# A two-matmul SiLU block on one core: first rows of x and first columns of w1 in smaller, interleaved pieces

## The chip, the core and the metric

The kernel runs on one core of one Trainium2 chip. The core has five engines with a program of their own each: TensorE (PE in the profile, its weight loads PEld), VectorE (DVE), ScalarE (ACT), GpSimd (POOL) and SyncE (SP). They meet only at semaphores. DMAs are issued from SP's and ACT's programs into one queue each (q1 and q10 in the profile). The metric is the device time of one execution in microseconds; lower is better.

## The reference

`x` is 1 x 2048 x 640, `w1` is 640 x 1728, `w2` is 1728 x 640, all bfloat16:

```python
def reference(x, w1, w2):
    h = jnp.einsum("bsd,df->bsf", x, w1)
    h = _silu(h)                      # h * sigmoid(h)
    out = jnp.einsum("bsf,fd->bsd", h, w2)
    return out
```

## The kernel before

TensorE contracts over the partitions, so the first product needs x transposed: 640 = 5 slices (DT) of 128 contraction rows. The 1728 columns of w1 are 13 full column blocks of 128 (ft 0 to 12) and a tail of 64. The 2048 rows of x are four chunks (sc) of 512.

**Getting x transposed.** Chunks 1 to 3 are transposed by the DMA itself (line 224, five per chunk, on SP's queue). Chunk 0 would come too late that way: its 512 rows are loaded as they are into x0_sb (line 206 on SP: rows 0 to 255; line 401 on ACT: rows 256 to 511), and TensorE transposes them by a matmul with the identity, in row blocks j of 128, five matmuls each (line 295). DVE copies three of a block's five results to xT_sb (line 468), ACT the other two (line 416).

**Loading w1.** In four groups of column blocks, 0-1, 2-3, 4-7 and 8-13. Group 0 is issued by ACT behind x's second half (line 406), groups 1 to 3 by SP (line 213), after SP has waited until x's first half has landed. SP then waits for group 2 before it issues the transposes, with the loads of w2 behind those of chunk 2.

**Warm-up.** TensorE first runs nine 512-column matmuls on z_sb, a tile of zeros (line 277), whose halves POOL (line 184) and DVE (line 463) write; it waits for both. Then it waits for POOL's identity.

**First product.** A unit is one column block times 512 rows: five accumulating matmuls (line 350) into one of four PSUM banks; ACT takes the sigmoid (line 426), DVE multiplies it with the sum and writes hT_sb, h transposed (line 490). In chunk 0, column blocks 0 and 1 are taken in two halves of 256 rows, first both blocks for rows 0 to 255, then both for the rest; the others take 512 rows. The 64-column tails of two chunks share one unit (line 339, lines 426 and 481), after chunks 1 and 3. On each engine the units are in one order.

**Second product.** For each of 16 row tiles of 128, 14 pairs of matmuls (line 388), 512 and 128 output columns wide; DVE copies the 512 (line 503), ACT the 128 (line 438) to one of four output buffers, SP stores (line 259). The last two tiles are taken together: first both of their 512-column parts, copied by DVE (line 515) and stored by SP (line 265), then both of their 128-column parts, copied by ACT (line 450) and stored by ACT (line 455).

The order of the work is written out by hand per engine, with a semaphore count at each wait. SP's head:

```python
            sp.wait_ge(sem_x0[0], 16)
            for gi in range(N_W1_ACT, len(w1_groups)):
                load_w1_group(gi)
```

Of the kernel before, what the change touches and what calls it, by code (L numbers as in the profile page):

```python
# [6 lines left out]
ALU = mybir.AluOpType  # L7


def bass_standalone__dense_activation_silu__prompt_kernel(  # L10
# [13 lines left out]
    P = 128  # L24
    assert D % P == 0 and S % 512 == 0 and 512 < D <= 1024
    DT = D // P
    FT = (F + P - 1) // P
    FP = FT * P
    F_LAST = F - (FT - 1) * P
    ST = S // P  # L30
    SCH = 512
    NSC = S // SCH
    JB = SCH // P
    NB1 = 4
    NOB = 4
    DA = 512
    DB = D - DA
    assert ST >= 4 and ST % 2 == 0 and (ST - 2) % NOB + 1 == (ST - 1) % NOB
    assert JB % 2 == 0

    w1_groups = [(0, 2), (2, 4), (4, 8), (8, FT)]
    N_W1_ACT = 1
    W1_BIG = 2

    def w1_group_of(ft):
        for gi, (a, b) in enumerate(w1_groups):
            if a <= ft < b:
                return gi
        raise AssertionError

    HN = SCH // 2
    N_SPLIT_FT = 2
    units = []
    for ft in range(N_SPLIT_FT):
        units.append((0, ft, 0, HN))
    for ft in range(N_SPLIT_FT):
        units.append((0, ft, HN, HN))
    PACK_TAIL = (F_LAST <= 64) and (FT >= 2)
    FT_REG = FT - 1 if PACK_TAIL else FT
    for ft in range(N_SPLIT_FT, FT_REG):  # L60
        units.append((0, ft, 0, SCH))
    for sc in range(1, NSC):
        for ft in range(FT_REG):
            units.append((sc, ft, 0, SCH))
        if PACK_TAIL and sc % 2 == 1:
            units.append((-1, sc - 1, sc, 0))
    if PACK_TAIL and NSC % 2 == 1:
        units.append((-1, NSC - 1, None, 0))
    NU = len(units)

    def unit_chunks(u):
        if u[0] == -1:
            return [c for c in (u[1], u[2]) if c is not None]
        return [u[0]]

    dve_incs = [len(unit_chunks(u)) if u[0] == -1 else 1 for u in units]
    dve_val = []
    acc = 0
    for inc in dve_incs:
        acc += inc  # L80
        dve_val.append(acc)
    chunk_done_cnt = {}
    for i, u in enumerate(units):
        for c in unit_chunks(u):
            chunk_done_cnt[c] = dve_val[i]
    def tail_half(sc):
        if not PACK_TAIL:
            return 0
        if NSC % 2 == 1 and sc == NSC - 1:
            return 0  # L90
        return sc % 2

    n_w2_full = FT - 1 if F_LAST != P else FT
    w2_half = n_w2_full // 2
    n_w2_dmas = (4 if (F - (FT - 1) * P) <= 64 else 3) if n_w2_full != FT else 2
    N_INIT = 3 + (1 if (not PACK_TAIL and FP != F) else 0)
    N_PAD = 1 if (PACK_TAIL or FP != F) else 0
    N_WARM_MM = 9
    TPV = 3
    assert TPV <= 4 and DT - TPV <= 4  # L100

    TP_BANKS = {0: (1, 0), 1: (1, 8), 2: (0, 8), 3: (1, 0)}

    def tp_slot(j, dt):
        which, base = TP_BANKS[j % 4]
        slot = base + dt if dt < TPV else base + 4 + (dt - TPV)
        return which, slot

    with ExitStack() as es:
# [3 lines left out]
        def ps(name, shape, dtype):  # L113
            return es.enter_context(nc.psum_tensor(name, shape, dtype))

        def sem(name):
            return es.enter_context(nc.semaphore(name))

        xT_sb = sb("xT_sb", [P, DT, S], bf16)
        w1_sb = sb("w1_sb", [P, DT, FP], bf16)  # L120
        w2_sb = sb("w2_sb", [P, FT, D], bf16)
        hT_sb = sb("hT_sb", [P, FT, S], bf16)
        sig_sb = sb("sig_sb", [P, NB1, SCH], bf16)
        o_sb = sb("o_sb", [P, NOB, D], bf16)
# [3 lines left out]
        z_sb = sb("z_sb", [P, SCH], bf16)  # L128
        ps1 = ps("ps1", [P, NB1, SCH], fp32)
        ps2 = ps("ps2", [P, 2, 1024], fp32)  # L130
        tp_views = [
            ps1[:, :, :].rearrange("p a (k s) -> p (a k) s", s=P),
            ps2[:, :, :].rearrange("p a (k s) -> p (a k) s", s=P),
        ]

        sem_init = sem("sem_init")
        sem_w2pad = sem("sem_w2pad")
        sem_z = sem("sem_z")
        sem_x0 = [sem(f"sem_x0_{i}") for i in range(JB // 2)]
        sem_x = [None] + [sem(f"sem_x{i}") for i in range(1, NSC)]  # L140
        sem_w1 = [sem(f"sem_w1_{i}") for i in range(len(w1_groups))]
        sem_w2 = sem("sem_w2")
        sem_o = [sem(f"sem_o{i}") for i in range(NOB)]
        sem_tp = sem("sem_tp")
        sem_tpc_v = sem("sem_tpc_v")
        sem_tpc_a = sem("sem_tpc_a")
        sem_pe1 = sem("sem_pe1")
        sem_act1 = sem("sem_act1")
        sem_dve1 = sem("sem_dve1")
        sem_pe2 = sem("sem_pe2")  # L150
        sem_ev_v = sem("sem_ev_v")
        sem_ev_a = sem("sem_ev_a")
        sem_ofin = sem("sem_ofin")
        block = es.enter_context(nc.Block())
# [3 lines left out]
        w2_full_v = w2[0:n_w2_full * P, :].rearrange("(ft p) d -> p ft d", p=P)  # L158

        segs = []  # L160
        for st in range(ST - 2):
            b2 = st % 2
            segs.append([(st, 0, b2, 0, DA), (st, 1, b2, DA, DB)])
        sA, sB = ST - 2, ST - 1
        segs.append([(sA, 0, 0, 0, DA), (sB, 0, 0, 512, DA)])
        segs.append([(sA, 1, 1, 0, DB), (sB, 1, 1, 512, DB)])
        grp_order = []
        for seg in segs:
            for g in seg:
                grp_order.append((g[0], g[1]))  # L170
        grp_idx = {g: i + 1 for i, g in enumerate(grp_order)}
        seg_done_idx = {}
        for seg in segs:
            last = max(grp_idx[(g[0], g[1])] for g in seg)
            for g in seg:
                seg_done_idx[(g[0], g[1])] = last
        grp_loc = {}
        for seg in segs:
            for (st, ci, b2, c0, ncol) in seg:
                grp_loc[(st, ci)] = (b2, c0, ncol)  # L180

        @block.gpsimd
        def _(pool):
            pool.memset(z_sb[:, SCH // 2:SCH], 0.0).then_inc(sem_z, 1)  # L184
            pool.memset(ident[:, :], 0.0).then_inc(sem_init, 1)
            pool.wait_ge(sem_init, 1)
            pool.affine_select(
                out=ident[:, :],
                in_=ident[:, :],
                compare_op=ALU.not_equal,  # L190
                fill=1.0,
                base=0,
                pattern=[[-1, P]],
                channel_multiplier=1,
            ).then_inc(sem_init, 1)
            pool.memset(warm_sb[:, :], 0.0).then_inc(sem_init, 1)
            if PACK_TAIL:
                pool.memset(hT_sb[:, FT - 1, :], 0.0).then_inc(sem_w2pad, 1)  # L198
            elif FP != F:
                pool.memset(w1_sb[:, :, F:FP], 0.0).then_inc(sem_init, 1)  # L200
                pool.memset(w2_sb[:, FT - 1, :], 0.0).then_inc(sem_w2pad, 1)

        @block.sync
        def _(sp):
            hj = JB // 2
            sp.dma_start(
                out=x0_sb[:, 0:hj, :], in_=x0_v[:, 0:hj, :]
            ).then_inc(sem_x0[0], 16)

            def load_w1_group(gi):  # L210
                a, b = w1_groups[gi]
                f0, f1 = a * P, min(b * P, F)
                sp.dma_start(
                    out=w1_sb[:, :, f0:f1], in_=w1_v[:, :, f0:f1]
                ).then_inc(sem_w1[gi], 16)

            sp.wait_ge(sem_x0[0], 16)
            for gi in range(N_W1_ACT, len(w1_groups)):
                load_w1_group(gi)

            def x_chunk_transposes(sc):
                s0 = sc * SCH
                for dt in range(DT):
                    sp.dma_start_transpose(
                        out=xT_sb[:, dt, s0:s0 + SCH],
                        in_=xf[s0:s0 + SCH, dt * P:(dt + 1) * P],
                    ).then_inc(sem_x[sc], 16)

            sp.wait_ge(sem_w1[W1_BIG], 16)
            for sc in range(1, NSC):  # L230
                x_chunk_transposes(sc)
                if sc == min(2, NSC - 1):
                    sp.dma_start(
                        out=w2_sb[:, 0:w2_half, :], in_=w2_full_v[:, 0:w2_half, :]
                    ).then_inc(sem_w2, 16)
                    sp.dma_start(
                        out=w2_sb[:, w2_half:n_w2_full, :],
                        in_=w2_full_v[:, w2_half:n_w2_full, :],
                    ).then_inc(sem_w2, 16)
                    if n_w2_full != FT:  # L240
                        if PACK_TAIL:
# [305 lines left out]
```

## Time and profile before

| what | value |
|---|---|
| time, median of 3 runs | 130.99 us (130.43 to 130.99) |
| span of the profiled execution | 128.5 us (the page has no other time of that execution) |
| PE busy | 124.7 us, 97%, 767 matmuls |
| DVE / ACT busy | 52.1 us / 39.5 us |
| first product (lines 350 and 339) | 6.17 to 64.99 us |
| second product (line 388) | 64.99 to 125.97 us |
| DMA | 9.87 MB, 77 GB/s over the span |

The span runs from the first to the last instruction; the times of runs also hold what lies around it. A line of the timeline has the start, the duration, the engine, the line of the kernel, the operation, output <- input, their shapes and, in brackets, the idle time before it with what ended it; merged instructions have a count xN, and their duration goes from the first start to the last end. A line of the chain has start, duration and what ran. Matmuls are pipelined, so the duration of one is its latency; how far apart they start says how fast they go. Times of DMA issues are from the start of the issuing instruction to the moment when the semaphore shows the data landed.

### The profile page before, as it was taken

Reading aid. Unit: us, or ns where it says so; the run is one execution under the profiler, and the core shown is the slowest. Engines: PE = TensorE matmul, PEld = TensorE weight load, DVE = VectorE, ACT = ScalarE, POOL = GpSimd, SP = SyncE. Lnnn points to the kernel's source line nnn. Section 1 sums busy time; section 2 is a strip of 40 time slices with the busy share of each in tenths; the row PEclk is TensorE's granted clock in tenths of the full one; section 3 lists DMA queues with packets and bytes.
Section 4 is the critical chain, followed back from the end, with each engine's and each line's share of the span. In section 5 each row is a group of like instructions: output and inputs, shape, how many; then the busy total and the mean of one; then the engine's idle time right before and its main releaser. Section 6 shows DMA issues by size and latency. Waiting matters only on the chain.

```text
span 128.5 us, 1884 instructions
## 1 busy us (share of the span) xinstructions
PE 124.7 (97%) x767; PEld 63.9 (50%) x767; DVE 52.1 (41%) x78; ACT 39.5 (31%) x77; POOL 2.8 (2%) x9
## 2 busy tenths in 40 slices
PE   6999999999999999999999999999999999999992
PEld 2574444444444444444455555555555555555461
DVE  0475666666676666666662210222220122221021
ACT  4355555555555555555520000000000000000001
POOL 7000000000000000000000000000000000000000
PEclk9999999999999999999999999999999999999999
DMA  3897463599900000000000111111011111011103
GB/s 100 258 367 207 109 96 87 98 355 347 195 8 5 0 3 0 0 0 0 0 5 15 36 51 51 56 51 48 3 51 51 56 51 51 12 39 56 51 0 102
DMA packets 15752, 9.87 MB, mean 77 GB/s; under 512 B 8832, under 2 KB 15744, under 8 KB 15744
## 3 DMA queue, kind: packets, MB, share of 16 engines
q1 hardware_dynamic: 14544, 9.03, 24.8%
q10 hardware_dynamic: 1200, 0.72, 1.8%
q8 instruction: 6, 0.10, 0.3%
q14 instruction: 2, 0.02, 0.0%
HBM read 5.16 MB, written 2.62 MB: 61 GB/s over the span
## 4 chain that ended last, share of the span: by engine, by line
PE 97%; ACT 1%; POOL 0%; issue 0%; POOLq 0%
PE ps L388 47%; PE ps L350 44%; PE ps L277 3%; PE ps L339 2%; PE ps L295 1%; ACT xT_sb L416 1%; ACT o_sb L450 0%; POOL z_sb L184 0%; POOLq L532 0%
## 5 line engine op out<-in xcount | busy, mean ns | idle before, releaser
L388 PE MATMUL ps<-w_sb,hT_sb 128*128 128x512 bf16 (+1 forms) x448 | 61.0, 299 | 0.0
L350 PE MATMUL ps<-xT_sb,w_sb 128*128 128x512 bf16 (+1 forms) x270 | 56.5, 371 | 0.0
L388 PEld LDWEIGHTS ps<-w_sb,hT_sb 128*128 128x128 bf16 x448 | 34.4, 98 | 26.8 <-issue 0.4
L490 DVE TENSOR_TENSOR hT_sb<-ps,sig_sb 128x512 bf16<-128x512 f32 (+1 forms) x54 | 36.3, 672 | 19.9 <-ACT sig_sb L426 19.4
L350 PEld LDWEIGHTS ps<-xT_sb,w_sb 128*128 128x128 bf16 x270 | 26.2, 98 | 29.9 <-issue 0.4
L426 ACT ACTIVATE sig_sb<-ps 128x512 bf16<-128x512 f32 (+1 forms) x56 | 32.6, 582 | 26.5 <-PE ps L350 25.3
L503 DVE CAST o_sb<-ps 128x512 bf16<-128x512 f32 x14 | 9.7, 692 | 42.3 <-PE ps L388 42.3
L438 ACT CAST o_sb<-ps 128x128 bf16<-128x128 f32 x14 | 3.7, 266 | 49.3 <-PE ps L388 49.3
L277 PE MATMUL ps<-z_sb 128*128 128x512 bf16 x9 | 3.4, 557 | 1.1 <-POOL z_sb L184 1.1
L468 DVE CAST xT_sb<-ps 128x384 bf16<-128x384 f32 x4 | 1.9, 549 | 4.1 <-PE ps L295 4.1
L515 DVE CAST o_sb<-ps 128x1024 bf16<-128x1024 f32 x1 | 1.2, 1225 | 5.4 <-PE ps L388 5.4
L481 DVE TENSOR_TENSOR hT_sb<-ps,sig_sb 64x512 bf16<-64x512 f32 x4 | 2.8, 689 | 1.1 <-ACT sig_sb L426 1.0
L450 ACT CAST o_sb<-ps 128x256 bf16<-128x256 f32 x1 | 0.4, 373 | 7.3 <-PE ps L388 7.3
L277 PEld LDWEIGHTS ps<-z_sb 128*128 128x128 bf16 x9 | 1.1, 136 | 2.9 <-issue 1.8
L339 PE MATMUL ps<-xT_sb,w_sb 128*64 128x512 bf16 x20 | 2.5, 384 | 0.0
L416 ACT CAST xT_sb<-ps 128x256 bf16<-128x256 f32 x4 | 1.3, 373 | 1.9 <-PE ps L295 1.9
L410 ACT ACT_TABLE_LOAD x1 | 1.3, 1283 | 1.8 <-issue 1.8
L198 POOL MEMSET hT_sb<- 128x2048 bf16 x1 | 1.8, 1805 | 0.0
L339 PEld LDWEIGHTS ps<-xT_sb,w_sb 128*64 128x64 bf16 x20 | 1.0, 109 | 1.5 <-issue 0.8
L295 PE MATMUL ps<-ident,x_sb 128*128 128x128 bf16 x20 | 1.4, 219 | 0.2 <-ACT xT_sb L416 0.2
L295 PEld LDWEIGHTS ps<-ident,x_sb 128*128 128x128 bf16 x20 | 1.1, 97 | 0.8 <-issue 0.5
L463 DVE MEMSET z_sb<- 128x128 uint32 x1 | 0.2, 165 | 0.8 <-PEq L532 0.8
(9 smaller groups left out, 1.6 us busy)
## 6 DMA issues: line engine op xcount, KB each, us to landing
out_dram<-o_sb SPq DMA_DIRECT2D x14, 160.0 KB, 1.8
w_sb<-in_w_dram SPq DMA_DIRECT2D x1, 1120.0 KB, 8.1
w_sb<-in_w_dram SPq DMA_DIRECT2D x1, 960.0 KB, 5.6
w_sb<-in_w_dram SPq DMA_DIRECT2D x1, 880.0 KB, 7.2
w_sb<-in_w_dram SPq DMA_DIRECT2D x1, 640.0 KB, 5.5
x_sb<-in_x_dram SPq DMA_DIRECT2D x1, 320.0 KB, 3.7
x_sb<-in_x_dram ACTq DMA_DIRECT2D x1, 320.0 KB, 4.0
w_sb<-in_w_dram ACTq DMA_DIRECT2D x1, 320.0 KB, 4.5
```

The source lines that it names most:

```text
L277: pe.matmul(ps1[:, NB1 - 1, :], lhsT=z_sb[:, 0:P], rhs=z_sb[:, :], start=True, stop=True,)
L295: ins = pe.matmul(tp_views[wv][:, sl, :], lhsT=x0_sb[:, j, dt * P:(dt + 1) * P], rhs=ident[:, :], start=True, stop=True,)
L339: ins = pe.matmul(ps1[hh * 64:hh * 64 + F_LAST, buf, :], lhsT=w1_sb[:, dt, f0:f0 + F_LAST], rhs=xT_sb[:, dt, scc * SCH:(scc + 1) * SCH], s ...
L350: ins = pe.matmul(ps1[:, buf, 0:n], lhsT=w1_sb[:, dt, ft * P:(ft + 1) * P], rhs=xT_sb[:, dt, col0:col0 + n], start=(dt == 0), stop=(dt == ...
L388: ins = pe.matmul(ps2[:, b2, c0:c0 + ncol], lhsT=hT_sb[:, ft, st * P:(st + 1) * P], rhs=w2_sb[:, ft, d0:d0 + ncol], start=(ft == 0), stop= ...
L416: act.copy(out=xT_sb[:, TPV:DT, j * P:(j + 1) * P], in_=tp_views[wv][:, s0_:s0_ + (DT - TPV), :],).then_inc(sem_tpc_a, 1)
L426: act.activation(out=sig_sb[:, buf, 0:n], in_=ps1[:, buf, 0:n], func=ACT.Sigmoid,).then_inc(sem_act1, 1)
L438: act.copy(out=o_sb[:, ob, DA:D], in_=ps2[:, b2, c0:c0 + ncol]).then_inc(sem_ev_a, 1)
L468: dve.tensor_copy(out=xT_sb[:, 0:TPV, j * P:(j + 1) * P], in_=tp_views[wv][:, s0_:s0_ + TPV, :],).then_inc(sem_tpc_v, 1)
L481: dve.tensor_tensor(out=hT_sb[hh * 64:hh * 64 + F_LAST, FT - 1, scc * SCH:(scc + 1) * SCH], in0=ps1[hh * 64:hh * 64 + F_LAST, buf, :], in1 ...
L490: dve.tensor_tensor(out=hT_sb[:, ft, col0:col0 + n], in0=ps1[:, buf, 0:n], in1=sig_sb[:, buf, 0:n], op=ALU.mult,).then_inc(sem_dve1, 1)
L503: dve.tensor_copy(out=o_sb[:, ob, 0:DA], in_=ps2[:, b2, c0:c0 + ncol]).then_inc(sem_ev_v, 1)
```

## The change

The whole program is written anew as a list of operations, each with its engine and the operations it depends on; a small planner gives each engine its operations in list order, with a wait for every dependence that an earlier wait has not covered. The computation is the same. What differs:

- Warm-up: six matmuls instead of nine, on a constant of ones that exists before the kernel's own first instruction, without a wait. z_sb is gone.
- Loads: x's rows 0 to 127 on SP, rows 128 to 255 on ACT, then on SP w1 group 0, w1 group 1, x's rows 256 to 511, w1 groups 2 and 3. SP waits for none of them before it issues the next. The DMA transposes wait for w1 group 2, as before.
- Order on TensorE in chunk 0: row blocks 0 and 1 transposed; column blocks 0 and 1 for rows 0 to 127, then for rows 128 to 255 (matmuls of 128 columns); column block 2 for rows 0 to 255; row blocks 2 and 3 transposed; column block 3 for rows 0 to 255; column blocks 0 to 3 for rows 256 to 511; the other blocks with 512 rows. DVE, ACT follow in the same order.
- PSUM is one tile of eight banks, taken in turn by transposes, units and output tiles; the second of the two transposed pieces of a row block has its own bank. There were four banks for units, and two pairs for output tiles.
- o_sb holds all 16 output tiles; nothing waits for a store but the end.
- w1_sb has 1728 columns instead of 1792.

```diff
-        @block.sync
...
-            sp.dma_start(
-                out=x0_sb[:, 0:hj, :], in_=x0_v[:, 0:hj, :]
-            ).then_inc(sem_x0[0], 16)
...
-            sp.wait_ge(sem_x0[0], 16)
-            for gi in range(N_W1_ACT, len(w1_groups)):
-                load_w1_group(gi)
...
-            sp.wait_ge(sem_w1[W1_BIG], 16)
-            for sc in range(1, NSC):
-                x_chunk_transposes(sc)
...
-            pe.wait_ge(sem_z, 2)
-            for i in range(N_WARM_MM):
...
-            for j in range(JB):
-                transpose_block(j)
...
+class Plan:
...
+        def run(name, eng):
+            seen = {}
+            for op in self.ops:
+                if op.eng != name:
+                    continue
+                need = {}
+                for d in op.deps:
+                    need[d.sem] = max(need.get(d.sem, 0), d.value)
+                for s, v in need.items():
+                    if seen.get(s, 0) < v:
+                        eng.wait_ge(sems[s], v)
+                        seen[s] = v
+                ins = op.emit(eng)
+                if op.sem is not None:
+                    ins.then_inc(sems[op.sem], 16 if op.group else 1)
...
+        load_x0("sp", 0, 1)
+        load_x0("act", 1, 2)
+        load_w1("sp", 0)
+        load_w1("sp", 1)
+        load_x0("sp", 2, 4)
+        load_w1("sp", 2)
+        load_w1("sp", 3)
+        add("act", lambda e: e.activation(out=warm_sb[:, :], in_=warm_sb[:, :], func=ACT.Sigmoid), [warm])
+
+        ones = nc.const_aps.tensor(1.0, [P, SCH], bf16)
+        for i in range(N_WARM):
+            add("pe", lambda e: e.matmul(
+                ps[:, NBANK - 1, :], lhsT=ones[:, 0:P], rhs=ones, start=True, stop=True))
...
+        def transpose_x0(j):
+            b0, b1 = take_bank(), take_bank()
+            for dt in range(DT):
+                b, k = (b0, dt) if dt < TPV else (b1, dt - TPV)
+                deps = [x0_of[j], id_b] + bank_free[b]
+                pe = add("pe", lambda e, b=b, k=k, dt=dt: e.matmul(
+                    ps[:, b, k * P:(k + 1) * P], lhsT=x0_sb[:, j, dt * P:(dt + 1) * P],
+                    rhs=ident[:, :], start=True, stop=True), deps)
+            cols = slice(j * P, (j + 1) * P)
+            v = add("dve", lambda e: e.tensor_copy(
+                out=xT_sb[:, 0:TPV, cols],
+                in_=ps[:, b0, 0:TPV * P].rearrange("p (k s) -> p k s", s=P)), [pe])
+            a = add("act", lambda e: e.copy(
+                out=xT_sb[:, TPV:DT, cols],
+                in_=ps[:, b1, 0:(DT - TPV) * P].rearrange("p (k s) -> p k s", s=P)), [pe])
+            bank_free[b0], bank_free[b1] = [v], [a]
+            xT_ready[0, j] = [v, a]
...
+        def unit(sc, ft, c0, n):
+            b = take_bank()
+            cols = slice(sc * SCH + c0, sc * SCH + c0 + n)
+            for dt in range(DT):
+                pe = add("pe", lambda e, dt=dt: e.matmul(
+                    ps[:, b, 0:n], lhsT=w1_sb[:, dt, ft * P:(ft + 1) * P], rhs=xT_sb[:, dt, cols],
+                    start=(dt == 0), stop=(dt == DT - 1)),
+                    x_deps(sc, c0, n) + w1_deps(ft) + bank_free[b] if dt == 0 else ())
+            silu(b, [(slice(0, P), ft, cols)], n, pe)
...
+        transpose_x0(0)
+        transpose_x0(1)
+        for c in range(2):
+            for ft in range(2):
+                unit(0, ft, c * P, P)
+        unit(0, 2, 0, 2 * P)
+        transpose_x0(2)
+        transpose_x0(3)
+        unit(0, 3, 0, 2 * P)
+        for ft in range(4):
+            unit(0, ft, 2 * P, 2 * P)
+
+        for ft in range(4, FR):
+            unit(0, ft, 0, SCH)
```

## The prediction

> **What bounds the kernel now.** I read the chain that ended last first, in order of time. It is TensorE nearly from end to end:
>
> ```profile
> 1.10 3.44 PE ps L277 x9
> 4.54 0.45 PE ps L295 x5
> 5.02 0.66 ACT xT_sb L416 x2
> 5.71 0.45 PE ps L295 x5
> 6.17 28.26 PE ps L350 x140
> 34.43 1.20 PE ps L339 x10
> 35.63 28.16 PE ps L350 x130
> 63.79 1.20 PE ps L339 x10
> 64.99 60.97 PE ps L388 x448
> ```
>
> From 6.17 us to 125.97 us matmuls follow one another without a gap; in the groups by line, L350, L339 and L388 have 0.0 us idle before them. A change can win only in the 6.17 us ahead of the first real matmul, by making the stream shorter, or after its end. The stream keeps the same columns, and the end is unchanged. So I read the head next, by the timeline:
>
> ```profile
> 0.83 0.17 DVE L463 MEMSET z_sb<- 128x128 uint32 x1 [0.83 <-PEq L532]
> 1.93 0.15 PEld L277 LDWEIGHTS ps<-z_sb 128*128 128x128 bf16 x1 [0.28 <-issue]
> 2.36 0.15 PEld L277 LDWEIGHTS ps<-z_sb 128*128 128x128 bf16 x1 [0.28 <-issue]
> 4.54 1.00 PE L295 MATMUL ps<-ident,x_sb 128*128 128x128 bf16 x15
> 5.09 1.95 DVE L468 CAST xT_sb<-ps 128x384 bf16<-128x384 f32 x4 [4.09 <-PE ps L295]
> 7.34 2.06 DVE L490 TENSOR_TENSOR hT_sb<-ps,sig_sb 128x256 bf16<-128x256 f32 x4 [0.30 <-ACT sig_sb L426]
> 10.38 6.83 SPq L224 DMA_TRANSPOSE xT_sb<-in_x_dram  x5
> ```
>
> Warm-up matmuls start 0.43 us apart, half of full speed, until the last two (3.95 against 3.64 for their weight loads): the slow clock ended near 4.0 us, although the granted-clock column reads 1.00 throughout. At full clock a 128-column matmul takes 57 ns (15 in 1.00 us), a 256-column one 110 ns (20 in 2.2 us), a 512-column one 217 ns. Transposes began at 4.54; the copies of two row blocks on DVE, about 0.5 us each, gave the first unit at 6.17, 1.63 us later.
>
> Then the DMA issues, whose last column is the time from issue to landing:
>
> ```profile
> w_sb<-in_w_dram SPq DMA_DIRECT2D x1, 880.0 KB, 7.2
> w_sb<-in_w_dram SPq DMA_DIRECT2D x1, 640.0 KB, 5.5
> x_sb<-in_x_dram SPq DMA_DIRECT2D x1, 320.0 KB, 3.7
> x_sb<-in_x_dram ACTq DMA_DIRECT2D x1, 320.0 KB, 4.0
> w_sb<-in_w_dram ACTq DMA_DIRECT2D x1, 320.0 KB, 4.5
> w_sb<-in_w_dram SPq DMA_DIRECT2D x1, 320.0 KB, 3.2
> ```
>
> With issue times 0.74 (x, both), 1.25, 4.42, 4.9 and 5.4 us, x's halves land at 4.42 and 4.74, w1's groups at 5.75, 7.6, 10.4 and 12.6. The queues' packets in quarter-microsecond windows give when bytes stopped moving: SP's x at 3.95 (landing 0.45 later), ACT's x at 4.0 (0.7), w1 group 0 at 5.2 (0.55), group 1 at 6.85 (0.75), group 2 at 8.75 (1.63). So the lag between bytes and landing grows in a stream that stays full.
>
> **The change part by part.** Let T be when the second half of the first 512 rows (rows 256 to 511) is transposed and copied. Before, the first chunk's units end at 6.17 + 2.20 (four 256-column units) + 11 x 1.086 = 20.32 us. After, T is followed by four 256-column units (2.20) and nine full ones (9.77): the end is T + 11.97. Break-even is T = 8.35 us, and from there on the two kernels do the same.
>
> *Warm-up.* Its operand is a constant written ahead of the starting barrier, so it starts when DVE's first instruction did, 0.83 instead of 1.10. Six at 0.427 end at 3.4. z_sb's two memsets (0.31 and 0.17 us) go; the identity, finished at 1.7 before, comes earlier; all of that lies beside the loads. On ACT the function-table load (1.28 us, at 1.79 before) moves up behind a single DMA issue and is over by about 2.8, ahead of its first copy at 4.15.
>
> *First loads.* The first 128 rows go alone on SP. SP's first 124 packets had moved by 2.75, so 128 by 2.8; with lag 0.45 to 0.7 they land at 3.25 to 3.5, about when the warm-up ends. The second 128 rows, on ACT's queue, land near 3.9 (117 of ACT's packets by 3.5). Five transposes at half clock (107 ns) from 3.4, then the copy: DVE starts 4.15, ends 4.7; the second copy ends about 5.25. Group 0 of w1 now sits on SP behind 160 KB; 640 KB in all had moved by 4.0 before, and 512-byte rows move at 346 GB/s, so 4.2 plus lag 0.55: 4.75. First unit at 4.8, a lead of 1.37 us.
>
> *Narrow pieces.* 20 matmuls of 128 columns (1.14 us) replace 10 of 256 (1.10), and two 512-column units become four of 256 (2.20 for 2.17): 0.07 us more, and four more sigmoids and multiplies, beside TensorE. They end at 4.8 + 1.14 = 5.94, where unit (column 2, rows 0 to 255) waits for w1 group 1: 320 KB more at 346 GB/s from 4.2 is 5.15, plus 0.55 to 0.75, taken as 5.8. It runs 5.95 to 6.5.
>
> *The second half of x.* This load is moved behind two w1 groups on SP's queue, and the next instructions on TensorE's queue are its ten transposes: everything behind them waits. Its bytes end at 5.15 + 320 KB at 376 GB/s (the mean of 9 to 11 us) = 6.0. Its lag is on no row. Lower end 0.45 (first load: 6.45), upper end 1.63 (group 2, the row after 3.4 us of full stream: 7.65); this one comes after 4.2 us of stream, but group 1, with 0.75, had two loads behind it on the queue, as this has. I take 1.0, between the two and nearer to group 1: landing 7.0. Transposes to copied took 1.63, so T = 7.0 + 0.05 + 1.63 = 8.68.
>
> *DVE's order.* The copies of rows 256 to 511 stand on DVE and ACT behind the multiply and sigmoid of the unit at 5.95. From that unit's start: ACT 0.75 later, 0.38 of sigmoid, 0.42 of multiply, 0.04 between: the multiply ends 1.59 after, at 7.54, just ahead of the transposes' end (7.6). T is thus never under that unit's start + 1.59 + two copies (1.0) + 0.07. With group 1 landing at 5.6 at best, T is at least 8.26: the lead of 1.37 us is cut to 0.09 by this order alone.
>
> *The waits taken off SP.* Its six loads issue at about 0.5 us each from 0.74, done by 3.8. The DMA transposes of chunk 1 still wait for group 2: bytes end near 7.75, landing 8.8 to 9.4 against 10.4 before. TensorE wants group 2 at T + 2.2 = 10.9 and chunk 1 at 20.6; both are covered by over 1 us. If group 2's lag doubled it would land at 11.0 and cost 0.1.
>
> *Eight PSUM banks for four, a buffer per output tile, waits planned by a list.* No row of the matmuls shows them waiting for a bank or an output buffer, so nothing is won; per unit still one wait. SP's 15 final waits run (17 ns each where shown) while the last store lands (2.2 us). Nothing.
>
> **Sum.** T 8.68 against 8.35: +0.33 us. The page gives the span, 128.5 us, and no time around it; the median of the runs is 130.99, so 2.5 us lie outside and are taken as unchanged. 130.99 + 0.33 = 131.3. Between the ends of the lag: -0.09 (floor) to T = 9.33, +0.98.
>
> The Trainium skill (DMA: Bandwidth & Descriptors, Latency and other measured facts) puts the memory's latency at 0.2 us on average and 2 us at high load. The lags of 0.45 and 1.63 agree with its direction; by its 2 us the load would land at 8.0 and the sum, an estimate, would be +1.33.
>
> **The rivals.** (1) *The second half of x lands late, slower.* From a landing at 7.33 on (lag 1.33), TensorE's wait makes the loss over 0.65 us. At 7.65 it is +0.98, 132.0. For it: group 2's row. Against it: group 1's 0.75 with as many loads behind.
>
> (2) *The slow clock lasts longer.* Before, it ended after 2.9 us of unbroken matmuls; now only 2.56 us are issued, and TensorE waits near 4.6. If it lasts to 7 us, the 20 narrow matmuls take 107 ns each (2.14), the unit after them starts at 6.94, T = 6.94 + 2.66 = 9.60: +1.25, 132.2. It decides (over 0.65) from a slow clock lasting to 5.6 us. For it: the speed-up came only after the sixth warm-up here. Against it: 3.4 to 4.6 is mostly filled by transposes.
> The Trainium skill (TensorE: Matmul & The Clock Gate, Part 1) has a free-running window of about 3.4 us that must have been busy before the half rate ends. The trace's 4.0 us can't contradict it; by that rule the end differs from run to run, which is this rival.
>
> (3) *Faster by over 0.65 us.* T would have to be under 7.7, the unit with group 1 would start before 5.04, ahead of its bytes. Only shorter copies or an earlier stream from DMA could do it; or runs that scatter (130.43 to 130.99). At T = 7.6: 130.2.
>
> (4) *The change does nothing.* If the lag is 0.7 (landing 6.7), T is 8.35 and the earlier start is given back exactly: 131.0. It lies inside the forecast's range and has its chance there.
>
> **How the numbers follow.** 0.5% of 131 us is 0.65 us, about what a measurement tells from no change. Forecast (T from 8.0 to 9.0): 0.52, its own range 130.6 to 131.6. Rival 1: 0.28. Rival 2: 0.12. Rival 3: 0.08. So faster 0.08, same 0.52, slower 0.40. The range reaches 130.4 (floor less the scatter of 0.5) to 132.3 (rivals 1 and 2 at their prices).
>
> **What would show it.** Warm-ups of 128x512 at about 0.85, six; first w1 matmul near 4.8; TensorE idle before the second ten transposes, released by x's DMA, and again before the first 256-column unit of rows 256 to 511, released by DVE's copy near 8.7; from there no gap. 128-column w1 matmuls 57 ns apart if the clock is full, 107 if not. Wrong if group 2 or chunk 1 releases TensorE, if the stream after 65 us has gaps, or if the first half's data land over 0.5 us off.

## The result and the profile after

The changed kernel takes 131.71 us (median of 8 runs, 131.19 to 132.59), the kernel before 130.76 in the same series (130.43 to 130.99): ratio 1.0073, 95% interval 1.0049 to 1.0097. It is slower by 0.95 us. The profiled spans say the same: 129.4 us against 128.5. Ratios and medians, here and below, leave out three slow runs of turn_first's ten (133.41 to 133.86 us) and one of no_sp_wait's six (134.19), all at a granted clock of 0.987, and a ratio can differ a little from that of the medians.

The profiled run, 131.19 us, is the quickest of the eight. All runs whose span is on record, of every kernel here, lie 1.8 us above their span, so the profiled run of before, with 128.5, was one of about 130.3 and quick too.

The chain that ended last, in order of time, of the changed kernel (start, duration, what ran):

```profile
1.66 4.94 DMA w_sb<-in_w_dram
6.60 0.05 issue
6.64 0.73 PE ps L219 x5
7.40 0.39 ACT sig_sb L205
7.82 0.42 DVE hT_sb L208
8.24 0.94 DVE xT_sb L180 x2
9.23 2.36 PE ps L219 x20
11.64 10.74 PE ps L219 x49
```

Before, the chain was TensorE from 6.17 us on. Now its head is a load: w1 group 1, issued at 1.66, lands at 6.60. Column block 2's unit starts there; then its sigmoid, its multiply, and behind them on DVE the two copies of rows 256 to 511. Only at 9.23 does TensorE get the first 256-column unit of those rows. In the prediction's terms T is 9.23 us, where 8.35 would have been level: 0.88 us late, the whole loss in the span.

The first lines of the timeline that answer to those of before, and the landing times in windows around the issues (the last column, from the issue at 1.19, 1.66 and 2.21):

```profile
0.77 2.72 PE L166 MATMUL ps<-const-bfloat16-1.0 128*128 128x512 bf16 x6 [0.77 <-PEq L334]
3.65 1.25 PE L176 MATMUL ps<-ident,x_sb 128*128 128x128 bf16 x10 [0.17 <-DMA x_sb<-in_x_dram]
5.02 2.35 PE L219 MATMUL ps<-xT_sb,w_sb 128*128 128x128 bf16 x25
6.64 0.44 PEld L219 LDWEIGHTS ps<-xT_sb,w_sb 128*128 128x128 bf16 x5 [0.31 <-DMA w_sb<-in_w_dram]
7.47 0.73 PE L176 MATMUL ps<-ident,x_sb 128*128 128x128 bf16 x10
8.16 1.01 DVE L180 CAST xT_sb<-ps 128x384 bf16<-128x384 f32 x2
9.14 7.42 SPq L241 DMA_TRANSPOSE xT_sb<-in_x_dram  x5
9.23 7.11 PE L219 MATMUL ps<-xT_sb,w_sb 128*128 128x256 bf16 x41 [0.48 <-DVE xT_sb L180]
```

```profile
w_sb<-in_w_dram SPq DMA_DIRECT2D x1, 320.0 KB, 3.7
w_sb<-in_w_dram SPq DMA_DIRECT2D x1, 320.0 KB, 4.9
x_sb<-in_x_dram SPq DMA_DIRECT2D x1, 320.0 KB, 5.2
```

The first w1 matmul comes at 5.02, 1.15 us ahead of before, and the lead is more than given back: TensorE waits for group 1 (to 6.64), for x's rows (2.21 + 5.2 = 7.4) and for the copies (to 9.23). From there the matmuls go on as before. In the list of waits there is one more line, "PE ps L287 <- DVE hT_sb L208: 0.2", at the start of the second product. It is no wait: only 215 of the 224 wide matmuls of line 287 have a record, the first recorded one at 66.05 is the narrow half of a pair, and the missing wide one fits exactly in the 0.2 us between it and the tail unit's end.

### The profile page after: what moved, and what is told of

The parts are those of the page before. It is cut to its first block, busy times and chain, and to the rows that moved or that the text cites. A ratio compares the mean times of both kernels' runs of the same rounds, so it can differ in the third digit from the quotient of the medians.

```text
span 129.4 us, 1881 instructions
## 1 busy us (share of the span) xinstructions
PE 124.2 (96%) x770; PEld 65.1 (50%) x784; DVE 52.6 (41%) x82; ACT 40.3 (31%) x81; POOL 2.4 (2%) x7
## 4 chain that ended last, share of the span: by engine, by line
PE 90%; DMA 4%; DVE 2%; ACT 1%; issue 1%; SPq 1%
PE ps L287 47%; PE ps L219 42%; DMA w_sb<-in_w_dram 4%; PE ps L229 1%; DVE hT_sb L208 1%; ACT sig_sb L205 1%; DVE xT_sb L180 1%; SPq L152 0%; SPq L143 0%; ACT o_sb L310 0%
## 5 line engine op out<-in xcount | busy, mean ns | idle before, releaser
L287 PE MATMUL ps<-w_sb,hT_sb 128*128 128x128 bf16 (+1 forms) x439 | 60.4, 297 | 0.6 <-DVE hT_sb L208 0.2
L219 PE MATMUL ps<-xT_sb,w_sb 128*128 128x512 bf16 (+2 forms) x285 | 57.0, 358 | 1.0 <-DVE xT_sb L180 0.5
L208 DVE TENSOR_TENSOR hT_sb<-ps,sig_sb 128x512 bf16<-128x512 f32 (+3 forms) x62 | 39.6, 640 | 21.9 <-ACT sig_sb L205 21.3
L287 PEld LDWEIGHTS ps<-w_sb,hT_sb 128*128 128x128 bf16 x448 | 34.4, 98 | 26.8 <-issue 0.4
L219 PEld LDWEIGHTS ps<-xT_sb,w_sb 128*128 128x128 bf16 x290 | 27.5, 99 | 30.0 <-DVE xT_sb L180 1.1
L205 ACT ACTIVATE sig_sb<-ps 128x512 bf16<-128x512 f32 (+2 forms) x60 | 33.3, 554 | 27.1 <-PE ps L219 25.9
L166 PE MATMUL ps<-const-bfloat16-1.0 128*128 128x512 bf16 x6 | 2.7, 623 | 0.8 <-PEq L334 0.8
L176 PE MATMUL ps<-ident,x_sb 128*128 128x128 bf16 x20 | 2.0, 266 | 0.3 <-DMA x_sb<-in_x_dram 0.2
L166 PEld LDWEIGHTS ps<-const-bfloat16-1.0 128*128 128x128 bf16 x6 | 0.7, 133 | 1.9 <-issue 1.9
```

The source lines that it names most:

```text
L166: add("pe", lambda e: e.matmul(ps[:, NBANK - 1, :], lhsT=ones[:, 0:P], rhs=ones, start=True, stop=True))
L176: pe = add("pe", lambda e, b=b, k=k, dt=dt: e.matmul(ps[:, b, k * P:(k + 1) * P], lhsT=x0_sb[:, j, dt * P:(dt + 1) * P], rhs=ident[:, :], ...
L205: a = add("act", lambda e: e.activation(out=sig_sb[:, s, 0:n], in_=ps[:, b, 0:n], func=ACT.Sigmoid), [pe, sig_free[s]])
L208: v = add("dve", lambda e, rows=rows, ft=ft, cols=cols: e.tensor_tensor(out=hT_sb[rows, ft, cols], in0=ps[rows, b, 0:n], in1=sig_sb[rows, ...
L219: pe = add("pe", lambda e, dt=dt: e.matmul(ps[:, b, 0:n], lhsT=w1_sb[:, dt, ft * P:(ft + 1) * P], rhs=xT_sb[:, dt, cols], start=(dt == 0), ...
L287: pe = add("pe", lambda e, ft=ft, t=t, b=b, c0=c0, d0=d0, n=n: e.matmul(ps[:, b, c0:c0 + n], lhsT=hT_sb[:, ft, t * P:(t + 1) * P], rhs=w2_ ...
```

## The experiments

My theory after the profile: T is set by late landings, and by column block 2's unit standing ahead of the copies on DVE. Rivals: the rewriting itself costs; the new loads are harmless and only the order is bad (or the reverse); a load is late because of what is queued behind it; the half-speed clock of TensorE lasts longer. Ratios below are to the kernel before in the same series.

**old_head: the new program with the head of before.**

```diff
-        load_x0("sp", 0, 1)
-        load_x0("act", 1, 2)
-        load_w1("sp", 0)
-        load_w1("sp", 1)
-        load_x0("sp", 2, 4)
+        load_x0("sp", 0, 2)
+        load_x0("act", 2, 4)
+        load_w1("act", 0)
+        load_w1("sp", 1, [x0_of[0]])
...
-        N_WARM = 6
+        N_WARM = 9
...
+        for j in range(JB):
+            transpose_x0(j)
+        for c in range(2):
+            for ft in range(2):
+                unit(0, ft, c * 2 * P, 2 * P)
...
```

> The new program (planner, eight banks, 16 output tiles, constant warm-up) with the head of before: x in two halves on SP and ACT, w1 group 0 on ACT, SP's wait for x, four transposed row blocks first, 256-column halves, nine warm-ups. If the whole loss lies in the order of loads and pieces, it is level with before: ratio 0.998 to 1.002, first w1 matmul at 6.0 to 6.2 us, end of the first product at 64.9. If the rewriting costs something by itself (waits, banks), it keeps part of the loss: ratio 1.004 or more with an end of the first product late or gaps after 20 us.

130.56 us, ratio 0.9977 (0.9961 to 0.9992). The planner, the eight banks, the 16 output tiles and the constant warm-up cost nothing; together they are worth about 0.3 us. In its profiled run (130.57) the first w1 matmul came at 6.42, later than expected, because part of the transposes ran at half speed (20 in 1.71 us). The loss lies in the loads and the order of chunk 0.

**hold_back: nothing queued behind the loads that matter.**

```diff
-        load_w1("sp", 2)
+        load_w1("sp", 2, [x0_of[2]])
```

> The changed kernel, but SP issues w1 groups 2 and 3 only when x's rows 256 to 511 have landed. Theory A (a load's lag grows with what is queued behind it): group 1's lag falls from 1.4 us to 0.75 or less, it lands near 6.0 instead of 6.6, x's rows near 6.7 instead of 7.4, and the copies of rows 256 to 511 end near 8.7 instead of 9.2; group 2, issued at 6.7 instead of 2.8, lands at 11 to 12, at or after the 10.9 where TensorE wants it, so the time is 131.2 to 132.3. Rival (the lag is made by the bytes ahead or by the length of the stream): group 1 and x land as before the edit (6.6 and 7.4), copies end at 9.2, and group 2 late costs up to 1 us on top: 132.3 to 133.

131.40 us, ratio 1.0039 (1.0023 to 1.0055). In its profiled run (131.18) group 1 landed at 6.5 and x's rows at 7.3, 0.1 earlier than in the change's; T was 9.14. So in these two runs what stands behind a load does not make it late, and theory A's mechanism did not come. Group 2, issued at 7.33, landed 4.0 us later, at 11.35, and held TensorE's weight loads for only 0.16 us, where the rival had up to 1 us: alone, it is much quicker than in the stream (6.3). The total lies in A's range, and its ratio is below the change's 1.0073 (1.0049 to 1.0097) with intervals that hardly overlap. Whether holding back helps in the change's slower runs, which were not profiled, is open. What the lag consists of, the busy share by half-microseconds of this run shows (columns: TensorE, its weight loads, DVE, ACT, POOL, granted clock, DMA share, GB/s):

```profile
5.00:5.50 0.50, 0.36 (x7) 0.39 (x8) 0.14 (x1) 0.00 (x0) 0.00 (x0) 1.00 1.04 349
5.50:6.00 0.50, 0.50 (x13) 0.50 (x11) 0.07 (x1) 0.38 (x2) 0.00 (x0) 1.00 0.92 328
6.00:6.50 0.50, 0.42 (x8) 0.24 (x5) 0.50 (x3) 0.50 (x3) 0.00 (x0) 1.00 0.30 106
6.50:7.00 0.50, 0.44 (x4) 0.41 (x5) 0.50 (x3) 0.23 (x1) 0.00 (x0) 1.00 0.12 44
7.00:7.50 0.50, 0.41 (x6) 0.14 (x4) 0.06 (x1) 0.19 (x1) 0.00 (x0) 1.00 0.00 0
```

With only these loads in the queues, most DMA engines are done near 6.0, but a share of 0.12 of 16, some two engines' worth, works on until just before 7.0, and the semaphore is full at 7.3. The packets' sizes (512 bytes for w1's rows, 1,280 for x's) tell the loads apart: w1's last packet moved at 6.14 and group 1 landed at 6.51, x's last at 6.95 and it landed at 7.33. The change's own run has 6.23 and 6.60, 6.99 and 7.41. So a load lands about 0.4 us after its own last packet, and the rest of the lag, some 0.8 us, is the time by which its last packets come behind the mean of the 16 engines. The Trainium skill (DMA: Bandwidth & Descriptors, Why a DMA increments its semaphore by 16 and not by 1) says the engines finish independently and only the full 16 means that all data has landed; the tail agrees. Which engines are behind, and why, stays open.

**x2_on_act: x's rows 256 to 511 on the other queue.**

```diff
         load_x0("act", 1, 2)
+        load_x0("act", 2, 4)
...
-        load_x0("sp", 2, 4)
```

> The changed kernel with x's rows 256 to 511 on ACT's queue right behind rows 128 to 255, instead of behind two w1 groups on SP's. They should land near 5.6 instead of 7.4, w1 group 0 somewhat later (5.3 for 4.9), group 1 about as now (6.6), since as many bytes are ahead of it. If the landing of x is what sets the start of the last four pieces, it gains 0.6 to 0.9 us: 130.8 to 131.1. If the unit of column block 2, which waits for group 1 and stands ahead of the copies on DVE, is what sets it, nothing is won: copies end at 9.2, time 131.6 to 131.8.

132.45 us, ratio 1.0112 (1.0074 to 1.0150). x's rows landed at 1.2 + 5.1 = 6.3 instead of 7.4, and T became later, 9.83. The chain of this run says why:

```profile
1.65 5.55 DMA w_sb<-in_w_dram
7.25 0.73 PE ps L219 x5
8.00 0.39 ACT sig_sb L205
8.42 0.42 DVE hT_sb L208
8.84 0.94 DVE xT_sb L180 x2
9.83 26.10 PE ps L219 x130
```

Both queues share the bandwidth, so what x gained, w1 lost: group 0 held TensorE until 5.90 (it landed at 4.89 in the change), group 1 came at 7.20. T follows column block 2's unit by 2.58 us again (2.59 in the change), whatever x does. I had expected no gain; not seen was that the ratio came out 0.004 above the change's, some 0.5 us, with intervals that overlap. The Trainium skill (the same page, Issuing engines are not separate DMA queues) says that loads from several queues run on the same 16 engines and interleave, and this run agrees.

**turn_first: the transposes ahead of column block 2's unit.**

```diff
-        unit(0, 2, 0, 2 * P)
         transpose_x0(2)
         transpose_x0(3)
+        unit(0, 2, 0, 2 * P)
```

> The changed kernel with row blocks 2 and 3 transposed and copied ahead of the unit of column block 2 instead of behind it, loads as in the change. If that unit's chain over ACT and DVE is the only cause, the copies end 0.5 us or more earlier, time 131.2 or less. If x's landing at 7.4 is just as late, the copies end at 7.4 + 1.7 = 9.1 and the two units for rows 0 to 255 come after the transposes: time 131.5 to 131.8, no gain.

131.43 us, ratio 1.0039 (1.0022 to 1.0056). That lies between the two cases expected, and against the change's 1.0073 (1.0049 to 1.0097) the intervals touch only at their ends: a gain of some 0.4 us is likely, not shown. So column block 2's unit is not the only cause. In the profiled run, one of 132.09 us, x landed even later, at 8.0, and group 1 at 7.2, where the change's run has 7.4 and 6.6; the chain goes through x's load. That run also shows the clock:

```profile
5.48 2.29 PE L219 MATMUL ps<-xT_sb,w_sb 128*128 128x128 bf16 x20 [0.53 <-ACT xT_sb L183]
8.07 0.97 PEld L176 LDWEIGHTS ps<-ident,x_sb 128*128 128x128 bf16 x10 [0.57 <-DMA x_sb<-in_x_dram]
```

Twenty 128-column matmuls in 2.29 us are half speed (1.29 in other runs), and the transposes at 8.07 still are, 0.97 for ten against 0.56.

**nine_warm: no gap after the warm-up.**

```diff
-        N_WARM = 6
+        N_WARM = 9
```

> The changed kernel with nine warm-up matmuls instead of six, so that TensorE has no gap between 3.4 us and the first transposes. If the half-speed clock in some runs is what scatters the changed kernel upward (131.2 to 132.6), the scatter shrinks to 131.2 to 131.8 with the median at 131.3 to 131.5; the copies of rows 256 to 511 still end near 9.2, since the loads set them. If the clock plays no part: same median and scatter as the change, 131.7 and up to 132.6.

131.83 us (131.62 to 132.17), ratio 1.0074 (1.0059 to 1.0089). The scatter shrank from 1.4 to 0.55 us, which fits the clock, but six and eight runs do not prove it. The median did not move. That does not clear the clock, since the edit costs time of its own: in the profiled run T was 9.66, and its chain goes through the nine warm-ups, transposes that begin at half speed, a copy and the pieces up to column block 2's unit, although group 1 had landed near 6.55:

```profile
0.77 4.00 PE ps L166 x9
4.77 0.55 PE ps L176 x5
5.34 0.57 DVE xT_sb L180
5.96 1.85 PE ps L219 x25
```

That the half clock is not the loss in the change's profiled run is shown by that run's own chain, which begins with group 1's load, and by the 0.31 us for which the weight loads stood for it. For its slower runs the clock stays a rival.

**no_sp_wait: loads without waits, alone, in the kernel before.**

```diff
-            sp.wait_ge(sem_x0[0], 16)
             for gi in range(N_W1_ACT, len(w1_groups)):
```

> The kernel before with one thing removed: SP's wait for x's first half ahead of w1 groups 1 to 3. One part of the change alone. If loads without a wait only compete with the loads that are needed first, w1 group 0 and x's second half land 0.3 to 0.8 us later than 5.75 and 4.74 and the first w1 matmul moves from 6.2 to 6.3 to 6.8: ratio 1.001 to 1.005. If the queues serve them in order of need, the first matmul stays at 6.2 and nothing changes: ratio 0.999 to 1.001; group 2 lands at 9 or earlier instead of 10.4 in both.

132.25 us, ratio 1.0127 (1.0085 to 1.0169): one removed wait costs 1.3 us between the medians, more than I expected at worst. w1 group 0 (ACT's queue, issued at 1.25) landed after 6.6 us instead of 4.5, and in the timeline TensorE, with all of x transposed, stands 1.26 us for it:

```profile
w_sb<-in_w_dram SPq DMA_DIRECT2D x1, 320.0 KB, 5.1
w_sb<-in_w_dram ACTq DMA_DIRECT2D x1, 320.0 KB, 6.6
```

```profile
8.03 5.80 PE L349 MATMUL ps<-xT_sb,w_sb 128*128 128x256 bf16 x36 [1.26 <-DMA w_sb<-in_w_dram]
```

SP's wait was what kept the later groups from sharing the bandwidth with the first.

**old_order: the change's loads with the order of before.**

```diff
-        transpose_x0(0)
-        transpose_x0(1)
-        for c in range(2):
-            for ft in range(2):
-                unit(0, ft, c * P, P)
-        unit(0, 2, 0, 2 * P)
...
+        for j in range(JB):
+            transpose_x0(j)
+        for c in range(2):
+            for ft in range(2):
+                unit(0, ft, c * 2 * P, 2 * P)
+
+        for ft in range(2, FR):
```

> The changed kernel's loads with the order of before: all four row blocks transposed first. TensorE's queue then stands at row block 2 until x's second half lands at 7.3 to 7.4, the first w1 matmul comes near 8.0 and the rest follows without a gap: 1.8 to 2 us over before, ratio 1.013 to 1.016. If the loads of the change were harmless and its order the cost, the ratio would be near 0.998.

134.56 us, ratio 1.0279 (1.0245 to 1.0313): twice the expected loss. In the profiled run (135.04) x's rows landed at 8.0, 0.6 us later than expected, and TensorE stood 3.1 us for them. Most of what is beyond that is the clock:

```profile
8.04 1.25 PE L176 MATMUL ps<-ident,x_sb 128*128 128x128 bf16 x10 [3.09 <-DMA x_sb<-in_x_dram]
10.39 0.38 ACT L205 ACTIVATE sig_sb<-ps 128x256 bf16<-128x256 f32 x1 [0.69 <-PE ps L219]
11.46 0.38 ACT L205 ACTIVATE sig_sb<-ps 128x256 bf16<-128x256 f32 x1 [0.68 <-PE ps L219]
12.53 0.38 ACT L205 ACTIVATE sig_sb<-ps 128x256 bf16<-128x256 f32 x1 [0.68 <-PE ps L219]
13.33 0.38 ACT L205 ACTIVATE sig_sb<-ps 128x256 bf16<-128x256 f32 x1 [0.42 <-PE ps L219]
```

The 256-column units end 1.07 us apart, half speed (0.55 in the change), until about 12.8; the first 140 matmuls with w1 take 29.90 us on the chain, against 28.26 before. The granted-clock column says 1.00 all the while. The Trainium skill (TensorE: Matmul & The Clock Gate, Part 1) has the half rate end only after a busy window of about 3.4 us; a 3.1 us gap before 8.04 and full speed after 4.7 us of matmuls agree with that; the 2.9 us of matmuls after which it ended in the kernel before are less than the page says.

**order_old_loads: the change's order with the loads of before.**

```diff
-        load_x0("sp", 0, 1)
-        load_x0("act", 1, 2)
-        load_w1("sp", 0)
-        load_w1("sp", 1)
-        load_x0("sp", 2, 4)
+        load_x0("sp", 0, 2)
+        load_x0("act", 2, 4)
+        load_w1("act", 0)
+        load_w1("sp", 1, [x0_of[0]])
...
-        N_WARM = 6
+        N_WARM = 9
```

> The changed kernel's order of pieces on TensorE, DVE and ACT with the loads of before (SP's wait included) and nine warm-ups. If the copies of rows 256 to 511 come 2.66 us after the start of column block 2's unit, and that unit starts when w1 group 1 lands, then with group 1 at 7.6 instead of 6.6 the copies end near 10.3 although x has landed at 4.7: about 2 us over before, ratio 1.013 to 1.017. If x's landing sets them, they end before 8 and the ratio is 0.995 to 1.000.

132.17 us, ratio 1.0103 (1.0083 to 1.0123). x had landed by 4.7, the chain still went through group 1:

```profile
4.29 3.25 DMA w_sb<-in_w_dram
7.59 0.73 PE ps L218 x5
8.34 0.39 ACT sig_sb L204
8.76 0.42 DVE hT_sb L207
9.18 0.94 DVE xT_sb L179 x2
10.17 26.10 PE ps L218 x130
```

The ratio is below the forecast, since the span of before that it was reckoned from is that of a quick run. T is the unit's start plus 2.58 us, for the third time, and the span, 130.3, is 1.8 us over before's, which is T less 8.35. With either set of loads the change's order is slow, because it hangs the transposes and copies of rows on a load that they do not need; with the loads of before the rows were there by 4.7 and that load came at 7.54. With either order the change's loads are slow too (old_order): the two parts of the change need each other, and together do not reach the old pair.

**swap_loads and swap_six: x's rows ahead of group 1.** Transposes ahead of column block 2's unit, too; nine warm-ups in swap_loads, six in swap_six.

```diff
-        load_w1("sp", 1)
         load_x0("sp", 2, 4)
+        load_w1("sp", 1)
...
-        unit(0, 2, 0, 2 * P)
         transpose_x0(2)
         transpose_x0(3)
+        unit(0, 2, 0, 2 * P)
```

> The changed kernel with x's rows 256 to 511 ahead of w1 group 1 on SP's queue, their transposes ahead of the unit of column block 2, and nine warm-ups. If a landing is set by the bytes ahead of it, x lands near 6.6 and group 1 near 7.4; copies end at 8.3, the two units for rows 0 to 255 at 8.5, the first chunk at 20.5: ratio to before 1.000 to 1.003. If x's load lands at 7.3 or later wherever it stands, the copies end at 9 and more and the ratio stays at 1.005 or above.

> The swap_loads kernel with the change's six warm-ups instead of nine. x's second half landed at 5.8 there and the transposes stood behind the warm-ups, so the first w1 matmul should come at 5.0 instead of 6.0 and the copies of rows 256 to 511 end at 8.0 to 8.3 instead of 9.1; the units of column blocks 2 and 3 then wait for group 1 at 7.3 and end at 8.4: ratio 0.996 to 0.999. If the gap after six warm-ups keeps the clock slow, the scatter is wider (over 1 us) and the ratio 1.000 to 1.005.

swap_loads: 130.81 us, ratio 0.9998 (0.9979 to 1.0016). swap_six: 131.22 us, ratio 1.0029 (1.0007 to 1.0052). In swap_loads the loss of the change is gone by the times, though not as reckoned. Its profiled run, 131.13, is the third slowest of twelve, with a span only 0.1 us under the change's: x landed after 4.1 us, at 5.8 and not 6.6, but the nine warm-ups and then first pieces that began at half speed held the transposes until 7.36, and T was 9.14. What its quicker runs do differently no profile shows. In swap_six the transposes came at 6.08 and the copies ended at 7.8, a little ahead of the 8.0 to 8.3 expected, but group 1, now behind x, landed at 7.9 instead of 7.3 (7.0 in swap_loads), and TensorE waited for it:

```profile
6.08 0.72 PE L176 MATMUL ps<-ident,x_sb 128*128 128x128 bf16 x10
6.79 1.01 DVE L180 CAST xT_sb<-ps 128x384 bf16<-128x384 f32 x2
8.03 6.67 PE L219 MATMUL ps<-xT_sb,w_sb 128*128 128x256 bf16 x45 [1.23 <-DMA w_sb<-in_w_dram]
```

So a landing isn't set by the bytes ahead alone: third on SP behind the same loads, 320 KB of x (rows of 1,280 bytes) landed at 5.8 in both these kernels, and 320 KB of w1 (rows of 512 bytes) at 6.5 to 7.2 in the change, hold_back, nine_warm, turn_first and old_order.

**narrow_old: only the narrow first pieces.** old_head, with column blocks 0 and 1 of rows 0 to 255 in pieces of 128 rows.

```diff
         for c in range(2):
             for ft in range(2):
-                unit(0, ft, c * 2 * P, 2 * P)
+                unit(0, ft, c * P, P)
+        for ft in range(2):
+            unit(0, ft, 2 * P, 2 * P)
```

> The old_head kernel with one part of the change: column blocks 0 and 1 of rows 0 to 255 in pieces of 128 rows, behind all four row blocks' transposes. Loads as in before. If the narrow pieces are worth something where no later load holds TensorE back, the first w1 matmul comes at 5.6 to 5.8 instead of 6.2 to 6.4 (first copy of DVE at 5.6, w1 group 0 at 5.6 to 5.75) and the rest follows without a gap: ratio to before 0.993 to 0.996, 130.0 to 130.3. If the second copy or DVE's order takes it back: ratio as old_head's 0.998.

130.40 us (129.99 to 130.87), ratio 0.9956 (0.9941 to 0.9971): faster than both kernels, by 0.6 us against before, and inside the forecast. About half of that is old_head's already, and the two intervals overlap (old_head's is 0.9961 to 0.9992), so what the narrow pieces are worth alone is not shown. The profiled run was its slowest, at half clock through all 20 transposes, and the chain is TensorE alone:

```profile
0.77 4.00 PE ps L165 x9
4.77 2.12 PE ps L175 x20
6.89 28.11 PE ps L218 x150
```

Even so its first w1 matmul is at 6.70, not at the expected 5.6 to 5.8; no profile of a run with the full clock there was taken, so where the 0.6 us of the median comes from in detail is argued and not shown.

## Why the prediction was right and where it was not

131.71 lies in the range, 130.4 to 132.3, and the kernel is slower, as the sum had it; but the sum's loss was 0.33 us, too small to measure, and 0.95 came. The likeliest case, no measurable change, is not what came; the nearest is rival 1, at 0.28: x's rows landing after 7.33 (7.41), at a loss of up to 0.98.

That it fits so well is in part luck. Rival 1 has x's landing set T, which by itself would have given 9.1. In the profiled run the copies waited longest for something else, the chain from w1 group 1 over column block 2's unit, which gave 9.23; that the two lie 0.13 us apart is chance. And that run is the quickest of eight: why the median run takes 0.5 us more is not shown, the scatter of the landings (below) and the clock being the candidates.

- *What bounds it.* Right: everything is in T, and the streams after it are the same (old_head's head in the new program is level or slightly better, 0.9977).
- *Warm-up.* 0.77 to 3.5 against 0.83 to 3.4. The half clock lasted until about 5.45 instead of 4.0 (weight loads 0.11 us apart until then, 0.06 from 5.51), just short of the 5.6 from which rival 2 decided. Its mechanism exists, as old_order shows; in the profiled run it isn't the loss, since TensorE waited for group 1 behind it.
- *First loads.* Rows 0 to 127 held the transposes until 3.65 (3.25 to 3.5 forecast), group 0 landed at 4.89 (4.75), first unit at 5.02 (4.8). Right within 0.25.
- *Narrow pieces.* 57 ns a matmul of 128 columns holds from 5.5 on; the first few ran at half speed, so the 20 took about 1.3 us instead of 1.14. The wait for group 1 hid that.
- *Landing of w1 group 1: the step that failed.* Taken as 5.8, it was 6.6. Counted by the queue's packets, its bytes had moved by 5.4 (5.15 forecast); the lag was 1.2 where I took 0.55 to 0.75 from before. The count is what misled: packets of later loads, moved by the engines that are ahead, stand in for its own last ones, which came at 6.23. I allowed a long lag to x's load, which was on the range's ends, and not to the load ahead of it, which was in the same stream.
- *Landing of x's second half.* 7.4 against 7.0: bytes by 6.15 (6.0 forecast), lag 1.25 against 1.0, the same cause. By itself it would have given T = 7.47 + 1.63 = 9.1, so the two nearly tie. In the profiled runs of the other kernels with these loads x landed between 7.3 and 8.0 and group 1 between 6.5 and 7.2, so both terms scatter, by as much as the loss itself.
- *DVE's order.* Right to 0.1 us: unit's start + 2.66 forecast, 2.58 to 2.59 measured in three kernels. With a start of 6.64 it gives the loss that came. The prediction had the chain and fed it too early a start. Its floor, T = 8.26, was also reckoned wrongly: it starts the unit at 5.6, but by the same working the pieces ahead of it end at 5.94, which makes the floor 8.60 and the least loss 0.25. So the range's lower part and rival 4's exact level were not possible by its own chain.
- *SP's waits taken off.* Group 2 landed at 9.14 (8.8 to 9.4) and the DMA transposes started with it. TensorE waited for neither. Right.
- *Time around the span.* I set the span of 128.5 against the median and had 2.5 us outside; all runs have 1.8. The profiled run of before was among its quickest. The difference of two spans (0.9) was safe from it, since both are of quick runs.

## What to carry to other kernels

A load that is issued early isn't a load that lands early: it shares the bandwidth with whatever is needed first, and it lands with its own last packets, which here came 0.8 us after the queue's count had its bytes moved. Put the loads in the order of need, and hold back by a wait what is needed later (removing one such wait cost 1.3 us here). When pieces are interleaved by hand, check on every in-order engine, not only on TensorE, what a copy stands behind: in order_old_loads the transposes of rows that had landed by 4.7 us waited until 8.0 behind a unit on TensorE, and their copies until 9.1 behind its multiply on DVE, for a load that neither needed.

## What the runs showed of the hardware that I had not expected

- The tail of a stream of loads: two engines' worth of work for almost a microsecond after the rest is done (hold_back, 6.0 to 7.0 us). A load landed 0.37 to 0.42 us after its own last packet in the runs of the change and of hold_back, with and without loads queued behind it.
- 320 KB in rows of 512 bytes landed 0.7 to 1.4 us later than 320 KB in rows of 1,280 bytes in the same place of the queue (five kernels against two, one profiled run of each). That the rows' length is the reason was not tested apart from the rest.
- The half clock isn't in the granted-clock column. It ended between 4.0 us (before) and about 12.8 us (old_order). The two latest ends, 9.0 in turn_first and 12.8, went with gaps in TensorE's work; but narrow_old, without a gap from 0.77 on, kept the half clock until 6.7.
